# A fused attention and GEGLU block: the last accumulator of a block moved SBUF to SBUF, TensorE's lists shaped by their place in the group, dense steps shared out over a block

## The chip, the cores and the metric

One core of a Trainium2 chip runs the whole program. The metric is the device time of one execution in microseconds (us); three executions were timed, and another was profiled.

## What is computed

A transformer block on x of 2048 x 512 in float32: layer norm, attention with 32 query heads of 16 that share one key and one value head, residual; layer norm, a gated feed-forward network (F = 1792), residual.

```python
def _A_ref(x, wq, wk, wv, wo):            # attention; H = 32, Dh = 16
    q = (x @ wq).reshape(B, S, H, Dh) -> B, H, S, Dh
    k = x @ wk
    v = x @ wv
    scores = jnp.einsum("bhqd,bkd->bhqk", q, k) * (Dh ** -0.5)
    p = _softmax(scores, axis=-1)
    o = jnp.einsum("bhqk,bkd->bhqd", p, v)
    return o -> (B, S, H * Dh) @ wo
def _B_ref(x, w_gate, w_up, w_down):
    return (_gelu(x @ w_gate) * (x @ w_up)) @ w_down
h = x + _A_ref(_layernorm(x, axis=-1), A_wq, A_wk, A_wv, A_wo)
h2 = h + _B_ref(_layernorm(h, axis=-1), B_w_gate, B_w_up, B_w_down)
```

## The kernel before, and what sets its order

**Tiling.** The 2048 queries are four blocks of 512. A block has eight groups of four heads, a group has 16 chunks of 128 keys. For each chunk there are two *scores* (line 352): each is two matmuls on the two row halves of TensorE into one of two score tiles of PSUM, followed on ScalarE by one exponential of 128 x 1024 (line 356). Scores are counted here from 0 to 1023, 256 to a block. When both exponentials of a chunk are done, the chunk is *weighed* with the values (line 360): four matmuls side by side in column quarters, in float32, into the group's accumulator. The values carry a column of ones, so the accumulator holds the softmax sums too.

**Dense work.** Everything behind the attention of a block (projection pp, gate pg, up pu, down pd) is a queue of products (`queue_products`). A product is split by the two row halves of TensorE: a *step* (`step`, line 772) issues one matmul of the first half and one, six steps late (LAG), of the second half, so that the two halves work at once. Each half of a product fills one of three PSUM banks, which VectorE empties when it is complete. A queue that runs dry lets the six late second halves run alone (`catch_up`), and the next start runs six first halves alone. Block b's dense work runs beside block b + 1's attention; that of the last block follows at the end (`last_dense`). Before the last block's own products, `rest` and the projections of the first three of four column pieces stand there as filling.

**The order.** TensorE, ScalarE and GpSimd run in the order of the code, and VectorE and the SP queue too. From score 279 on the loop over CYCLES writes that order as *lists*: a list weighs 3, 3 or 2 chunks at once and then runs a string in which s is a score and d a dense step. A cycle of three lists has 8 chunks, 16 scores and 11, 11 and 14 steps. Where fewer dense steps are ready than the string has, the list is *empty*: the steps that are there are run, and then the third string of the row, which weighs one chunk (v) and takes two scores in turn. A step of a block's first products is ready when `pieces` says that its quarter of the block's output is there.

**The end of a group.** `evacuate` copies the accumulator to SBUF (oT, line 373), writes it to DRAM (acc_d, line 422) and reads it back turned (oc, line 391), both on the SP queue; only the very last accumulator goes SBUF to SBUF (line 383, SP and ScalarE's queue). At a block's last group four `piece`s follow on VectorE, one for each quarter of the queries: reciprocal, product, and a split in two float32r parts (lines 396 to 126). `outs` holds these in pairs; one pair is taken out per list.

Of the kernel before, what the change touches and what calls it, by code (L numbers as in the profile page):

```python
# [50 lines left out]
BOUND_LISTS = (3, 4)  # L51
# [6 lines left out]
def kernel(  # L58
# [12 lines left out]
    nc = tc.nc  # L71
    x = x.flatten_outer_dims()
# [7 lines left out]
    NB = S // T  # L80
# [75 lines left out]
    def run(outer, first):  # L156
# [209 lines left out]

        def take_out():
            for step in outs.pop(0):
                step()

        def evacuate(b, g, acc):
# [47 lines left out]
            if b == NB - 1 and g == NG - 1:  # L419
                move_out()  # L420
            else:
                nc.sync.dma_start(acc_d[:, g % 4, :], oT)
                if b == 0 and g < NG - 1:
                    outs.append([turn_out])
                else:
                    turn_out()
            if b == NB - 1 and g == NG - 1:
                last_out.append(piece)
            elif b > 0 and g == NG - 1:
                outs.extend([partial(piece, t), partial(piece, t + 1)] for t in (0, 2))  # L430
            elif k == 1:

                outs.extend([[] for _ in range(4 if b == 0 else 1)])
                outs.extend([partial(invert, t), partial(invert, t + 1)] for t in (0, 2))
                outs.append([divide])
            if b == 0 and g == NG - 1:
                while outs:
                    take_out()
                pieces[b] = TB
# [95 lines left out]
        clock = 0  # L535
# [27 lines left out]
        def project(b, t):  # L563
# [27 lines left out]
            return f"pp_{b}_{t}", 3 * DC, terms, done, lambda: pieces.get(b, 0) > t  # L591
# [367 lines left out]

        def finish(n):  # L960
            for _ in range(min(n, len(pend))):
                pb, pg, pkc, pp, pacc, _ = pend.pop(0)
                weigh(pacc, pp, pkc)
                if pkc == KC - 1:
                    evacuate(pb, pg, pacc)
# [35 lines left out]
        n, lead = 0, 2 * PER + 23  # L1001
        with tc.manual_schedule(engines={mybir.EngineType.SP, mybir.EngineType.DVE}):
# [25 lines left out]
            def pace():  # L1028
                nonlocal n, parts, db, tiny
# [9 lines left out]
                n += 1  # L1039
                if n % 4:  # L1040
                    return
                if outs:
# [3 lines left out]
                if n == 2 * PER + 4:  # L1046
                    prime()
# [4 lines left out]
            while n < lead:  # L1052
                pace()
                if n % 4 == 2 and len(pend) > 2 and n < lead - 1:
                    finish(1)
                elif n % 4 == 0:
                    finish(len(pend) - 2)
        assert not outs
# [8 lines left out]
        def before(idle):  # L1067
            if outs:
                take_out()
            while (b_t := divmod(sum(turned.values()), TB)) in scaled_at:  # L1070
# [19 lines left out]
        for i in range(-((lead - end) // 16)):  # L1090
            if first and i in BOUND_LISTS:
                bound_flag(BOUND_LISTS.index(i))
            for count, woven, plain in CYCLES:
                idle = available() < woven.count("d")
                if idle:
                    while available():
                        step()
                    if at == len(queue) or queue[at][0].startswith("pg"):
                        catch_up()
                bent = before(idle)  # L1100
                if not idle:
                    finish(count)
                for key in bent:
                    later.extend(gate(*key))
                for move in plain if idle else woven:
                    if move == "d":
                        step()
                    elif move == "v":
                        finish(1)
                        clock += 4  # L1110
                    elif n < end:
                        score(n)
                        n += 1
                        clock += 1
# [337 lines left out]
```

## Time and profile before

| | us |
|---|---|
| three timed executions | 1417.53, 1417.65 (median), 1420.09 |
| profiled execution, its own time | 1417.39 |
| its span, first to last instruction | 1415.2 |
| TensorE busy in the span | 1388.3 (98%) |
| ScalarE busy | 1030.1 (73%) |
| VectorE busy | 632.7 (45%) |
| first and last exponential start | 53.7 and 1263.6 |

In a row of a timeline stand start and length in us, the engine, line, operation, what it writes and reads, and how many instructions were merged; in brackets the idle time before it and what ended it. In a row of windows stand the stretch, its length, the busy time of TensorE and of its weight loads with the number of instructions (further engines where no line is picked), the granted clock, the share of the DMA engines and their GB/s. Times count from the start of the span.

### The profile page before, as it was taken

Reading aid. Unit: us, or ns where it says so; the run is one execution under the profiler, and the core shown is the slowest. Engines: PE = TensorE matmul, PEld = TensorE weight load, DVE = VectorE, ACT = ScalarE, POOL = GpSimd, SP = SyncE. Lnnn points to the kernel's source line nnn. Section 1 sums busy time; section 2 is a strip of 40 time slices with the busy share of each in tenths; the row PEclk is TensorE's granted clock in tenths of the full one; section 3 lists DMA queues with packets and bytes.
Section 4 is the critical chain, followed back from the end, with each engine's and each line's share of the span. In section 5 each row is a group of like instructions: output and inputs, shape, how many; then the busy total and the mean of one; then the engine's idle time right before and its main releaser. Section 6 shows DMA issues by size and latency. Waiting matters only on the chain.

```text
span 1415.2 us, 25089 instructions
## 1 busy us (share of the span) xinstructions
PE 1388.3 (98%) x10384; PEld 752.6 (53%) x10384; DVE 632.7 (45%) x1043; ACT 1030.1 (73%) x1147; POOL 218.3 (15%) x305
## 2 busy tenths in 40 slices
PE   6999999999999999999999999999999999999998
PEld 5533333335455555555555555545555555557886
DVE  7412221214364354454354454445264453536665
ACT  6699999997777777777777777787778777752000
POOL 5576866630000000000000000000000000001000
PEclk9999999999999999999999999999999999999999
DMA  4466766645222333311432333311333332344352
GB/s 158 135 210 204 225 211 214 213 151 199 78 85 93 116 102 117 102 65 57 153 105 87 118 116 101 102 65 36 141 101 102 117 101 102 105 141 171 131 190 77
DMA packets 66850, 180.31 MB, mean 127 GB/s; under 512 B 9484, under 2 KB 9484, under 8 KB 66696
## 3 DMA queue, kind: packets, MB, share of 16 engines
q1 hardware_dynamic: 56768, 144.40, 31.0%
q0 software_dynamic: 9760, 34.08, 7.5%
q8 instruction: 84, 1.38, 0.4%
q14 instruction: 38, 0.31, 0.1%
q10 hardware_dynamic: 200, 0.14, 0.0%
HBM read 130.87 MB, written 47.45 MB: 126 GB/s over the span
## 4 chain that ended last, share of the span: by engine, by line
PE 93%; ACT 2%; DMA 1%; DVE 1%; issue 1%; SPq 0%; DVEq 0%; ACTq 0%
PE acc L360 32%; PE s L352 20%; PE pg L772 8%; PE pu L772 8%; PE pd L772 8%; PE pq L205 4%; PE pd L802 3%; PE pp L772 2%; PE pu L802 2%; PE pg L802 2%; ACT p L356 2%; DMA w<-w_d 1%; PE pk L1240 1%; PE pd_rest L814 1%; PE pxt L598 0%
## 5 line engine op out<-in xcount | busy, mean ns | idle before, releaser
L356 ACT ACTIVATE p<-s 128x1024 f32<-128x1024 f32 x1024 | 959.3, 1040 | 231.0 <-PE s L352 230.7
L360 PE MATMUL acc<-p,v_sb 128*32 128x512 f32 x4096 | 490.0, 598 | 0.0
L352 PE MATMUL s<-qg,kaug 50*128 50x512 f32 x1984 | 386.8, 427 | 4.0 <-ACT p L356 3.6
L352 PEld LDWEIGHTS s<-qg,kaug 50*128 50x128 f32 x1984 | 170.7, 184 | 287.8 <-issue 131.3
L360 PEld LDWEIGHTS acc<-p,v_sb 128*32 128x32 f32 x4096 | 110.2, 109 | 228.9 <-issue 215.7
L772 PE MATMUL pg<-x2h,w 64*128 64x512 f32 x672 | 173.8, 392 | 0.0
L772 PE MATMUL pu<-x2h,w 64*128 64x512 f32 x672 | 172.7, 391 | 0.0
L135 POOL TENSOR_SCALAR rstd<-mv 128x1 f32<-128x1 f32 x16 | 3.5, 220 | 964.8 <-DVE mv L133 964.7
L772 PE MATMUL pd<-w,gh 64*128 64x512 f32 x624 | 123.9, 392 | 1.4 <-DVE h L702 1.4
L702 DVE TENSOR_TENSOR h<-h,pd 128x512 f32<-128x512 f32 x80 | 54.4, 686 | 148.0 <-PE pd L772 148.0
L772 PEld LDWEIGHTS pg<-x2h,w 64*128 64x128 f32 x672 | 94.3, 185 | 11.9
L772 PEld LDWEIGHTS pu<-x2h,w 64*128 64x128 f32 x672 | 94.5, 186 | 11.0
L772 PE MATMUL pg<-x2l,w 64*128 64x512 f32 x336 | 99.3, 391 | 0.0
L772 PE MATMUL pu<-x2l,w 64*128 64x512 f32 x336 | 99.1, 391 | 0.0
L772 PEld LDWEIGHTS pd<-w,gh 64*128 64x128 f32 x624 | 68.2, 185 | 13.4 <-DVE h L702 2.7
L911 ACT ACTIVATE ga<-ga 128x512 f32<-128x512 f32 x14 | 8.8, 632 | 90.4 <-DVE ga L908 90.4
L396 DVE RECIPROCAL oc<-oc 128x128 f32<-128x128 f32 x64 | 56.6, 922 | 34.5 <-DMA oc<-acc_d 27.3
L772 PE MATMUL pd<-w,gl 64*128 64x512 f32 x312 | 71.8, 391 | 0.0
L639 DVE TENSOR_TENSOR g<-g,pg 128x512 f32<-128x512 f32 x42 | 28.8, 685 | 90.5 <-PE pg L772 90.5
L635 DVE COPY g<-pg 128x512 f32<-128x512 f32 x42 | 29.0, 692 | 72.2 <-PE pg L772 72.2
L639 DVE TENSOR_TENSOR u<-u,pu 128x512 f32<-128x512 f32 x42 | 28.8, 686 | 68.3 <-PE pu L772 68.3
L373 DVE COPY oT<-acc 128x512 f32<-128x512 f32 x32 | 22.1, 691 | 72.4 <-PE acc L360 72.4
(244 smaller groups left out, 1459.2 us busy)
## 6 DMA issues: line engine op xcount, KB each, us to landing
w<-w_d SPq DMA_DIRECT2D x112, 512.0 KB
w<-w_d SPq DMA_DIRECT2D x28, 1024.0 KB
qg<-q_d SPq DMA_DIRECT2D x62, 200.0 KB
q_d<-qh SPq DMA_DIRECT2D x32, 256.0 KB
acc_d<-oT SPq DMA_DIRECT2D x31, 256.0 KB
oc<-acc_d SPq DMA_DIRECT2D x124, 64.0 KB
w_d<-w_0b POOLq DMA_DIRECT2D x14, 512.0 KB, 5.8
w_d<-w_1b POOLq DMA_DIRECT2D x14, 512.0 KB, 6.3
```

Of the source, the lines that this page charges most:

```text
L205: nc.tensor.matmul(pq, wt[:, d, c * P : (c + 1) * P], xt[:, d, :], start=(n == 0), stop=(n == 3 * DC - 1),)
L352: nc.tensor.matmul(s[:, a, :], kaug[rows, kc * P : (kc + 1) * P], qg[rows, u, :], start=True, stop=True,)
L356: nc.scalar.activation(p[:, 2 * u : 2 * u + 2, :], s, AF.Exp, scale=SCALE)
L360: nc.tensor.matmul(acc[32 * j : 32 * j + 32, :], v_sb[:, kc, :], p[:, j, :], start=(kc == 0), stop=(kc == KC - 1), skip_group_check=True,)
L373: nc.vector.tensor_copy(oT, acc)
L396: nc.vector.reciprocal(oc[:, 1, sl], oc[:, 1, sl])
L635: nc.vector.tensor_copy(half, bank)
L639: nc.vector.tensor_tensor(half, half, bank, op=ALU.add)
L702: nc.vector.tensor_tensor(hs[b, t], hs[b, t], bank, op=ALU.add)
L772: nc.tensor.matmul(bank, lhsT[r], rhs[r], start=(k == 0), stop=(k == n - 1), skip_group_check=True,)
L802: nc.tensor.matmul(bank, lhsT, rhs, start=(i == 0), stop=(i == len(ts) - 1))
L814: nc.tensor.matmul(bank, lhsT, rhs, start=(i == 0), stop=(i == len(ts) - 1))
```

## The change

1. At the last group of *every* block the accumulator goes SBUF to SBUF, by eight transfers of 16 rows on the SP and the POOL queue (the very last: SP and ScalarE's). The pieces are taken out when a count of issued work (`clock`: 1 for a step or a score, 4 for a chunk) has gone on by 30, the second pair 20 later; a quarter's projection is ready 8 and 16 counts behind that.
2. Lists are made by place in the group (`shape`): weigh runs end at chunks 3, 6 and 8 of each eight, and the string of WOVEN is picked by how many scores are then due, so there are short ones too. Where no dense steps are ready, a list weighs one chunk and takes two scores, each with up to three spare steps.
3. `spread` counts the steps left until the next block's first product and the scores left for them, and takes d out of the longest run of a string when it has more than its share. In the last block 24 steps are kept back; all that is left runs behind the last weigh run.
4. The first stage hands over at score 263 instead of 279, and the first loads of the dense work (`prime`) are issued there.

```diff
-CYCLES = (
-    (3, "ssdddddsdddsddds", "vssvssvs"),
-    (3, "ssdddddsdddsddds", "vssvssvs"),
-    (2, "ssdddddsdddsdddsddds", "ssvssvss"),
+WOVEN = (
+    "ddd", "sddd", "sdddsdd", "ssddddds", "ssdddddsddds", "ssdddddsdddsddds",
+    "ssdddddsdddsdddsddds", "ssdddddsdddsdddsdddsddds",
 )
+BOUNDARIES = ((3, 6), (6, 5), (8, 7))
+MOVE, PIECE, PAUSE = 30, 8, 20
+OPEN, KEEP = 15, 24
...
             def move_out():
+                queues = nc.sync, nc.scalar if b == NB - 1 else nc.gpsimd
                 for half in (1, 0):
                     for j in range(4):
                         r0, r1 = 64 * k + DH * j, 32 * j + DH * half
-                        (nc.sync, nc.scalar)[j % 2].dma_start(
+                        queues[j % 2].dma_start(
...
-                pieces[b] = t + 1
+                pieces[b, t] = clock + PIECE * (1 + t % 2)
...
+            if g == NG - 1:
                 move_out()
+                if b == NB - 1:
+                    last_out.append(piece)
+                else:
+                    for t in (0, 2):
+                        outs.append((clock + MOVE, [partial(piece, t), partial(piece, t + 1)]))
+                return
...
-        n, lead = 0, 2 * PER + 23
+        n, lead = 0, 2 * PER + 7
...
+        def shape():
+            m = done_chunks % 8
+            edge, extra = next(x for x in BOUNDARIES if m < x[0])
+            count = min(edge - m, len(pend))
+            aim = 2 * (done_chunks + count) + (extra if count == edge - m else n - 2 * done_chunks)
+            return count, spread(WOVEN[min(aim, end) - n])
+
+        def spread(woven):
+            todo, i = left[0], at
+            while i < len(queue) and not (todo and i in heads):
+                todo += queue[i][1]
+                i += 1
+            b = heads.index(i) if i in heads else NB - 1
+            pairs = 2 * PER * (b + 1) + OPEN - n if b < NB - 1 else end - n
+            if b == NB - 1:
+                todo -= KEEP
+            most = -(-max(todo, 0) * woven.count("s") // pairs) if pairs > 0 else len(woven)
+            while woven.count("d") > most and "ddd" in woven:
+                run = max(woven.replace("s", " ").split(), key=len)
+                woven = woven.replace(run, run[1:], 1)
+            return woven
...
+        while n < end or pend:
...
+            count, woven = shape()
+            few = available() < woven.count("d")
+            bent = before(few and not available())
+            if few:
+                count, woven = 1, None
+            finish(count)
+            clock += 4 * count
...
+            if few:
+                for _ in range(2):
+                    next_pair()
+                    spare_steps(3)
+            else:
+                for move in woven:
+                    step() if move == "d" else next_pair()
+        while available():
+            step()
```

What this does to TensorE's order is best seen in three places. First, a full list inside a block: from the second score of the list that begins with score 359 to its third (s is a score, 1 row for its two matmuls; pu_.._0 is a matmul of the first row half, for an up product, pg_.._1 one of the second half, for a gate product). Before:

```order
L352 MATMUL s_0_4379<-qg_3_3883,kaug 128x512 x2
L772 MATMUL pu_4_0_4383<-x2h_3161,w_0_4_1_4250 128x512
L772 MATMUL pg_4_1_4338<-x2h_3161,w_0_4_0_4181 128x512
L772 MATMUL pu_4_0_4383<-x2l_3162,w_0_4_1_4250 128x512
L772 MATMUL pg_4_1_4338<-x2l_3162,w_0_4_0_4181 128x512
L772 MATMUL pu_4_0_4383<-x2h_3161,w_0_4_1_4250 128x512
L772 MATMUL pg_4_1_4338<-x2h_3161,w_0_4_0_4181 128x512
L772 MATMUL pu_4_0_4383<-x2h_3161,w_0_4_1_4250 128x512
L772 MATMUL pg_4_1_4338<-x2h_3161,w_0_4_0_4181 128x512
L772 MATMUL pu_4_0_4383<-x2l_3162,w_0_4_1_4250 128x512
L772 MATMUL pg_4_1_4338<-x2l_3162,w_0_4_0_4181 128x512
L352 MATMUL s_1_4394<-qg_3_3883,kaug 128x512 x2
```

And now:

```order
L357 MATMUL s_0_4461<-qg_3_3972,kaug 128x512 x2
L777 MATMUL pu_5_0_4465<-x2h_3174,w_0_5_1_4332 128x512
L777 MATMUL pg_5_1_4420<-x2h_3174,w_0_5_0_4261 128x512
L777 MATMUL pu_5_0_4465<-x2l_3175,w_0_5_1_4332 128x512
L777 MATMUL pg_5_1_4420<-x2l_3175,w_0_5_0_4261 128x512
L777 MATMUL pu_5_0_4465<-x2h_3174,w_0_5_1_4332 128x512
L777 MATMUL pg_5_1_4420<-x2h_3174,w_0_5_0_4261 128x512
L777 MATMUL pu_5_0_4465<-x2h_3174,w_0_5_1_4332 128x512
L777 MATMUL pg_5_1_4420<-x2h_3174,w_0_5_0_4261 128x512
L357 MATMUL s_1_4474<-qg_3_3972,kaug 128x512 x2
```

Five steps have become four; the gaps behind hold three, as before. In block 1's attention from score 359 to 519 the lists are so of 10, 10 and 12 steps (in the list of 14 the gap has three). In the two later blocks, from 567 to 727 and from 844 to 1004, they are of 11, 11 and 13.

Second, TensorE at the end of block 0, around score 270. Before, lists of one weighed chunk (acc) and two scores:

```order
L360 MATMUL acc_0_3120<-p_3210,v_sb 32x512 x4
L352 MATMUL s_0_3250<-qg_0_2879,kaug 128x512 x2
L352 MATMUL s_1_3254<-qg_0_2879,kaug 128x512 x2
L360 MATMUL acc_0_3120<-p_3223,v_sb 32x512 x4
L352 MATMUL s_0_3263<-qg_0_2879,kaug 128x512 x2
L352 MATMUL s_1_3267<-qg_0_2879,kaug 128x512 x2
```

And now (the same place; pp is the first projection of block 0):

```order
L365 MATMUL acc_0_3120<-p_3222,v_sb 32x512 x4
L357 MATMUL s_1_3260<-qg_0_2879,kaug 128x512 x2
L357 MATMUL s_0_3265<-qg_0_2879,kaug 128x512 x2
L777 MATMUL pp_0_0_3269<-wo_hi,o_hi_1607 128x512
L777 MATMUL pp_0_0_3269<-wo_lo,o_hi_1607 128x512
L777 MATMUL pp_0_0_3269<-wo_hi,o_lo_1608 128x512
L777 MATMUL pp_0_0_3269<-wo_hi,o_hi_1607 128x512
L777 MATMUL pp_0_0_3269<-wo_lo,o_hi_1607 128x512
L357 MATMUL s_1_3275<-qg_0_2879,kaug 128x512 x2
```

Block 0's dense work begins at score 271 instead of 281.

Third, TensorE from the last score (s_1) on. Before, the rest of the queue stands ahead of the last weigh run, and the last block's own projection (pp) right behind it:

```order
L772 MATMUL pd_12_1_1_13188<-w_2_6_12457,gl_6_12984 128x512
L772 MATMUL pd_12_1_1_13188<-w_2_6_12457,gh_6_12983 128x512 x2
L772 MATMUL pd_12_1_1_13188<-w_2_6_12457,gl_6_12984 128x512
L360 MATMUL acc_7_12761<-p_13138,v_sb 32x512 x4
L360 MATMUL acc_7_12761<-p_13158,v_sb 32x512 x4
L857 MATMUL pp_0_13235<-wo_hi,o_hi_10935 128x512
```

And now (the first rows of 27 steps that stand between the run and pp):

```order
L357 MATMUL s_1_13137<-qg_7_12376,kaug 128x512 x2
L365 MATMUL acc_7_12739<-p_13102,v_sb 32x512 x4
L365 MATMUL acc_7_12739<-p_13125,v_sb 32x512 x4
L777 MATMUL pd_8_1_0_13160<-w_2_4_11665,gh_4_12168 128x512
L777 MATMUL pd_8_0_1_13119<-w_2_5_12514,gh_5_12730 128x512
L777 MATMUL pd_8_1_0_13160<-w_2_4_11665,gh_4_12168 128x512
L777 MATMUL pd_8_0_1_13119<-w_2_5_12514,gh_5_12730 128x512
```

The last weigh run follows its last score at once, and 27 steps have moved behind it. Counted in the whole order, the nine stretches between scores 263, 311, 359, 519, 567, 727, 791, 844, 1004 and 1024 hold 72, 105, 320, 105, 350, 132, 119, 350 and 40 steps; before, 48, 105, 360, 97, 360, 120, 119, 360 and 51. The number of matmuls is the same.

More of the change, by code (lines that the diff above doesn't have):

```diff
@@ L363, in weigh @@
                 )
+        clock = out_at = 0
         def take_out():
-            for step in outs.pop(0):
+            for step in outs.pop(0)[1]:
                 step()
@@ L534, in run @@
         tanhs, later = [], []
-        clock = 0
         def new_xT(b):
@@ L589, in done @@
                     later.append(norm)
-            return f"pp_{b}_{t}", 3 * DC, terms, done, lambda: pieces.get(b, 0) > t
+            return f"pp_{b}_{t}", 3 * DC, terms, done, lambda: (
+                (b, t) in pieces and clock >= pieces[b, t] and (b, t) in xbs
+            )
         def turn(b, t):
@@ L1053, in run @@
                 pace()
[L1054 to L1058, printed above, removed]
+            prime()
         set_banks("ps_rest")
@@ L1089, in run @@
         )
[L1090 to L1114, printed above, removed]
+        def shape():
[4 more added lines that the diff above has]
+            return count, spread(WOVEN[min(aim, end) - n])
@@ new lines, in next_pair, with spare_steps @@
+        def next_pair():
+            nonlocal n, clock
+            if n < end:
+                score(n)
+                n += 1
+                clock += 1
+        def spare_steps(k):
+            nonlocal clock
+            for _ in range(k):
+                if available():
+                    step()
+                elif ahead and (at == len(queue) or queue[at][0].startswith("pg")):
+                    step(False)
+                else:
+                    clock += 1
+                    return
@@ L1115, in run @@
+        while available():
+            step()
         fixed.close()
```

51 lines of the change are left out of this document (27 added, 24 removed).

## The prediction

> **What bounds the kernel now.** I read the page first, its busy shares and its list of waits, then the stretches of the attention phase one by one, then single lists.
>
> ```profile
> PE 1388.3 (98%) x10384; PEld 752.6 (53%) x10384; DVE 632.7 (45%) x1043; ACT 1030.1 (73%) x1147; POOL 218.3 (15%) x305
> PE s L352 <- ACT p L356: 3.6, 10, 0.6
> PE pd L772 <- DVE h L702: 1.4, 3, 0.6
> ```
>
> TensorE is busy 98% of the span. In the view of who waited for whom (us in total, times, longest), it loses 3.6 us to exponentials that are not done and 1.4 us to VectorE that has not emptied a bank. So shifting dense steps can recover some 5 us at most; it removes no matmul. The question is whether it adds waits. The next view counts the dense matmuls (L772, two to a step) in nine stretches whose ends are starts of weigh runs: those at scores 259, 311, 359, 519, 567, 727, 791, 844, 1004 and 1024.
>
> ```profile
> 304.28:364.73 60.45, 14.85 (x96) 10.26 (x96) 1.00 0.43 142
> 364.73:424.92 60.19, 30.16 (x210) 20.78 (x210) 1.00 0.25 84
> 424.92:626.25 201.33, 100.87 (x720) 69.16 (x720) 1.00 0.31 101
> 626.25:687.46 61.21, 26.96 (x194) 18.43 (x194) 1.00 0.19 57
> 687.46:888.06 200.60, 99.99 (x720) 68.50 (x720) 1.00 0.35 118
> 888.06:966.99 78.93, 34.09 (x240) 23.42 (x240) 1.00 0.22 74
> 966.99:1036.19 69.20, 33.17 (x238) 22.70 (x238) 1.00 0.33 111
> 1036.19:1236.69 200.50, 100.31 (x720) 69.02 (x720) 1.00 0.31 101
> 1236.69:1265.79 29.10, 15.09 (x102) 10.51 (x102) 1.00 0.35 116
> ```
>
> Halved, the old steps are 48, 105, 360, 97, 360, 120, 119, 360, 51: 1620. By the new order they are 72, 105, 320, 105, 350, 132, 119, 350, 40, and 27 behind the last weigh run. So 71 steps arrive (24, 8, 12 and 27) and 71 leave (40, 10, 10 and 11). What is a step worth where it arrives, and where it leaves?
>
> **A full list from the inside.** Three lists in a row on TensorE: a weigh run (acc), two scores at once, then scores with dense steps between.
>
> ```profile
> 407.51 0.73 PE L352 MATMUL s<-qg,kaug 50*128 50x512 f32 x4
> ...
> 409.24 0.42 PE L352 MATMUL s<-qg,kaug 50*128 50x512 f32 x2
> ...
> 414.18 0.73 PE L352 MATMUL s<-qg,kaug 50*128 50x512 f32 x4
> 414.75 0.40 PE L772 MATMUL pg<-x2h,w 64*128 64x512 f32 x2
> ...
> 415.90 0.46 PE L352 MATMUL s<-qg,kaug 50*128 50x512 f32 x2
> ...
> 418.18 1.92 PE L360 MATMUL acc<-p,v_sb 128*32 128x512 f32 x16
> 420.03 0.74 PE L352 MATMUL s<-qg,kaug 50*128 50x512 f32 x4
> ...
> 421.75 0.42 PE L352 MATMUL s<-qg,kaug 50*128 50x512 f32 x2
> ```
>
> Five steps fill 414.75 to 415.90: 0.23 us a step. Meanwhile ScalarE takes the exponentials, five to a row here, the five of a list:
>
> ```profile
> 408.06 4.69 ACT L356 ACTIVATE p<-s 128x1024 f32<-128x1024 f32 x5 [1.97 <-PE s L352]
> 414.78 4.69 ACT L356 ACTIVATE p<-s 128x1024 f32<-128x1024 f32 x5 [1.53 <-PE s L352]
> 420.58 4.69 ACT L356 ACTIVATE p<-s 128x1024 f32<-128x1024 f32 x5 [1.10 <-PE s L352]
> L356 ACT ACTIVATE p<-s 128x1024 f32<-128x1024 f32 x1024 | 959.3, 1040 | 231.0 <-PE s L352 230.7
> ```
>
> One takes 1.04 us, and in a row they start (4.69 - 1.04) / 4 = 0.91 us apart. There are two score tiles, so the third score of a list needs the first exponential, the fourth the second. The first ends at 408.06 + 1.04 = 409.10, and the third score starts at 409.24, 0.14 us later; in the next list 415.82 and 415.90, 0.08 later; in the third 421.62 and 421.75, 0.13 later. How close may a score follow? Here is one that TensorE had to wait for, with its exponential, the second of this row:
>
> ```profile
> 322.71 0.50 PE L352 MATMUL s<-qg,kaug 50*128 50x512 f32 x2 [0.42 <-ACT p L356]
> 320.60 2.06 ACT L356 ACTIVATE p<-s 128x1024 f32<-128x1024 f32 x2
> ```
>
> It started 0.05 us behind the exponential's end (320.60 + 2.06 = 322.66). So the five steps are no filler: they last just as long as the score must wait anyway, and with four the third score can come only 0.09, 0.03 and 0.08 us earlier. Behind it three steps and a score take 4 x 0.23 = 0.92 us, again just the 0.91 of an exponential. **A step cut from the long gap gives back some 0.07 us, not 0.23; the rest becomes a wait.** The second step cut from the same gap gives nothing.
>
> **The change part by part.**
> - *Steps that leave full lists.* Scores 359 to 519: ten cycles with 10, 10 and 12 steps for 11, 11 and 14, each 0.09 + 0.03 + 0.08 = 0.2 us shorter: -2.0. In the two stretches of -10 only the list of 14 loses one: ten times 0.08, -0.8 each. Scores 311 to 359: three such, -0.2. Bounds for these 63 cuts: nothing given back (0) and all of it (63 x 0.23 = -14.5); I take the 3.8 that the three lists show.
> - *Steps that arrive.* At the first block end 24 x 0.23 = 5.5; there the lists of one weigh chunk and two scores, with no dense steps, become fewer. At the second 8 x 0.23 = 1.8. At the third 12 x 0.23 = 2.8, and eight more that were cut in that stretch's full lists and sit in its formerly empty ones, 8 x 0.16 = 1.3. Lists at the first and second end that are cut too: +0.9 of waits. Bounds: none of it hidden (as here), or half of it where a score waited.
> - *Waits that go.* What TensorE lost around the first end (305 to 372), the second (618 to 640; two rows) and the third (936 to 960; two rows):
>
> ```profile
> PE s L352 <- ACT p L356: 2.1, 5, 0.6
> PE s L352 <- ACT p L356: 0.4, 1, 0.4
> PE pd L772 <- DVE h L702: 0.3, 1, 0.3
> PE s L352 <- ACT p L356: 0.9, 3, 0.5
> PE pd L772 <- DVE h L702: 0.5, 1, 0.5
> ```
>
>   Half of the first stays, since six of twelve lists without dense steps stay: -1.0; at the second -0.7, at the third -1.4, together -3.1. Starts of weigh runs cancel: 157 lists before, 157 after.
> - *The end.* Rows of TensorE around the last weigh run, and the last place where it waits for VectorE's quarters:
>
> ```profile
> 1262.61 0.72 PE L772 MATMUL pd<-w,gh 64*128 64x512 f32 x3 [0.55 <-DVE h L702]
> ...
> 1265.79 1.92 PE L360 MATMUL acc<-p,v_sb 128*32 128x512 f32 x16
> 1267.65 0.50 PE L857 MATMUL pp<-wo_hi,o_hi 128*128 128x512 f32 x1
> ...
> 1281.92 0.50 PE L857 MATMUL pp<-wo_hi,o_hi 128*128 128x512 f32 x1 [0.29 <-DVE o_hi L125]
> ```
>
>   The last list loses seven steps, six unpaired half steps (three slots) and a wait: 10 x 0.23 + 0.55 = -2.9; the three lists before it -0.2. Behind the run stand 27 steps and the three slots: 30 x 0.23 = +6.9. The weigh run then waits for its last exponential, +0.5 (a score and its exponential less one chunk of 0.9). Six-step products side by side empty banks fast, and the last FFN chunk is projected only just ahead: +1.0, from 0 to 3. What they cover is little: TensorE works without a gap from 1267.65, and the quarters cost it 0.3 to 0.6: -0.5.
> - *SBUF to SBUF.* What the two routes take from the copy of the accumulator to the first reciprocal:
>
> ```profile
> 620.72 0.69 DVE L373 COPY oT<-acc 128x512 f32<-128x512 f32 x1 [1.28 <-PE acc L360]
> 627.38 0.95 DVE L396 RECIPROCAL oc<-oc 128x128 f32<-128x128 f32 x1 [0.20 <-issue]
> 1267.79 0.69 DVE L373 COPY oT<-acc 128x512 f32<-128x512 f32 x1 [1.20 <-PE acc L360]
> 1273.97 0.95 DVE L396 RECIPROCAL oc<-oc 128x128 f32<-128x128 f32 x1 [5.50 <-DMA oc<-oT]
> ```
>
>   5.97 us through DRAM, 5.49 directly. In the new order the quarters stand on VectorE where a count is reached, later than that at the second and third end (two lists, some 13 us); at the first they stand about where the data lands. I take 0; bounds -0.5 and, if the POOL queue is slow, +3 once. The Trainium skill, "DMA: Bandwidth & Descriptors", section "Anatomy of one DMA — SWDGE (gpsimd) path", gives each DMA a fixed cost of about 2.0 us; by it one leg less would be worth 2.0 at each of three ends, and the sum below would be an estimated 6 lower; the trace shows 0.5 between the routes.
> - *Two quarters at once between bank evictions.* The third quarter's reciprocal begins 3.57 us behind the first's:
>
> ```profile
> 630.95 0.94 DVE L396 RECIPROCAL oc<-oc 128x128 f32<-128x128 f32 x1
> ```
>
>   So a pair holds VectorE 3.6 us beside products that need banks; before, empty lists lay there. Bounds 0 and 2.5 at each of two ends; I take 0, since the products' steps are spaced by scores.
>
> **The sum:** leaving -2.0 - 0.8 - 0.8 - 0.2 = -3.8; arriving 5.5 + 1.8 + 2.8 + 1.3 + 0.9 = +12.3; waits -3.1; end -3.1 + 6.9 + 0.5 + 1.0 - 0.5 = +4.8. Together +10.2, less about 1 for the three or four arriving steps that fall into a score's wait (0.4 and 0.6 us in the rows above): **+9**. The profiled execution took 1417.39 us, so 1426.4; the median of the runs is 0.26 above it: **1426.6 us**, 0.6% slower.
>
> **The rivals.**
> 1. *The score could start earlier* (faster). If the third score followed its exponential by less than the 0.05 us seen, or exponentials ran faster with less beside them, a cut step would give back all of 0.23. It decides from a margin of 0.23 behind the exponential; the lists show 0.14, 0.08 and 0.13. Then leaving is -14.5, the waits that I put at 0.9 and 1.3 go, and the sum is -14.5 + 10.1 - 3.1 + 4.8 - 1 = -3.7: 1414.0. Against it: every one of the three lists. Chance 0.08.
> 2. *Half of that*: cut steps give back half, 1420 or so. Chance 0.09.
> 3. *New waits at the block ends*: quarters before evictions, a late POOL transfer or the last FFN chunk stall TensorE by 2.5 + 2.5 + 3 more: 1431 to 1435. For it: VectorE's 3.6 us; against it: 1.4 us of bank waits in the whole span. Chance 0.13.
> 4. *The clock falls.* The new waits come in nearly every list. In the first stretch TensorE waited most and its granted clock stood at 1.00, as in the others. The Trainium skill, "TensorE: Matmul & The Clock Gate", section "A second HAM failure mode: psum-queue depth-cycling", tells of frequent short idle times between groups that threw the clock between half and full; the trace does not agree, waits of up to 0.6 us left it at 1.00. Half a clock in the third stretch alone would add its 201 us. Chance under 0.01.
>
> **How the numbers follow.** The forecast, 1421 to 1431, has 0.69. The range reaches down to the half case and up into the third rival: 1418 to 1433, with about 0.83 inside. A measurement of this kernel tells 0.2% (2.8 us) from no change, so faster is below 1414.8 and slower above 1420.5. Faster: three quarters of the first rival, 0.06. Within: the rest of it and most of the second, 0.10. Slower: the forecast, the third and fourth and what is left of the second, 0.84.
>
> **What would show it.** In the new profile the scores' wait for exponentials should grow from 3.6 us to some 10, in many pieces of 0.1 to 0.2 between scores 359 and 519; a cycle there should last 19.8 to 19.9 us with four steps fewer, against 20.05 (200.50 us for ten in the stretch from 1036.19); the last weigh run should start some 4 us later, and the work behind it 5 to 7 us later still. If a cycle lasts 19.1, the first rival is right; if waits for VectorE grow by several us, the third.

## The result

The changed kernel takes 1435.49 us (median of 4 runs, 1433.06 to 1438.52) for 1417.7 us before: ratio 1.0123, 95% interval 1.0100 to 1.0145. It is 1.2% slower. The forecast was 1426.6 us with a range up to 1433, so the direction was right and the size was half of what came. The profiled execution took 1436.32 us (span 1434.5, granted clock 0.997).

### The profile after

The page's busy line, and then, from the view of who waited for whom (us in total, times, longest), the lines that answer to those of before:

```profile
PE 1405.6 (98%) x10384; PEld 753.1 (53%) x10384; DVE 639.3 (45%) x1052; ACT 1030.8 (72%) x1147; POOL 224.3 (16%) x317
```

```profile
PE s L357 <- ACT p L361: 4.6, 20, 0.6
PE pd L777 <- DVE gh L674: 1.0, 1, 1.0
PE pd L777 <- DVE h L707: 0.5, 1, 0.5
```

TensorE runs the same 10384 matmuls and is busy 17.3 us longer; its waits as this view counts them hardly grew. So the loss isn't where that view looks. It is found by stretches: the dense matmuls (L777) between the starts of the same weigh runs as before (scores 259, 311, 359, 519, 567, 727, 791, 844, 1004, 1024), with the length of each stretch in the second column and the granted clock in the third from the right:

```profile
303.56:369.83 66.27, 23.27 (x144) 15.64 (x144) 1.00 0.40 133
369.83:430.02 60.19, 29.48 (x210) 20.18 (x210) 1.00 0.29 93
430.02:630.19 200.17, 90.88 (x640) 60.54 (x640) 1.00 0.29 95
630.19:694.09 63.90, 29.64 (x210) 20.44 (x210) 1.00 0.17 50
694.09:894.83 200.74, 98.07 (x700) 67.25 (x700) 1.00 0.34 115
894.83:975.40 80.57, 37.36 (x264) 25.23 (x264) 1.00 0.25 80
975.40:1045.66 70.26, 33.66 (x238) 22.95 (x238) 1.00 0.32 105
1045.66:1246.19 200.53, 98.17 (x700) 67.06 (x700) 1.00 0.30 99
1246.19:1271.95 25.76, 11.27 (x80) 7.58 (x80) 1.00 0.21 69
```

Set against the nine stretches of before:

| stretch (scores) | steps | change, us |
|---|---|---|
| up to 259 | none | -0.72 |
| 259 to 311 | 48 to 72 | +5.82 |
| 311 to 359 | 105, 3 lists cut | 0.00 |
| 359 to 519 | 360 to 320 | -1.16 |
| 519 to 567 | 97 to 105 | +2.69 |
| 567 to 727 | 360 to 350 | +0.14 |
| 727 to 844 | 239 to 251 | +2.70 |
| 844 to 1004 | 360 to 350 | +0.03 |
| 1004 to 1024 | 51 to 40 | -3.34 |
| last weigh run to the end | 0 to 27 | +13.14 (149.41 to 162.55) |

Together +19.3, the difference of the two spans. Two things stand out: 60 steps left three stretches that got 0.99 us shorter between them, and the end, with 6.2 us of steps in it (27 x 0.23), got 13 longer.

### What a cut list looks like

The stretch that lost 40 steps, one list of 10 (four steps, three, three) on TensorE, and the exponentials beside it (rows left out are marked ...):

```profile
430.02 2.78 PE L365 MATMUL acc<-p,v_sb 128*32 128x512 f32 x24
432.73 0.73 PE L357 MATMUL s<-qg,kaug 50*128 50x512 f32 x4
...
434.35 0.49 PE L357 MATMUL s<-qg,kaug 50*128 50x512 f32 x2
...
435.38 0.40 PE L357 MATMUL s<-qg,kaug 50*128 50x512 f32 x2
...
436.30 0.40 PE L357 MATMUL s<-qg,kaug 50*128 50x512 f32 x2
```

```profile
433.27 4.69 ACT L361 ACTIVATE p<-s 128x1024 f32<-128x1024 f32 x5 [1.47 <-PE s L357]
```

The first exponential ends at 433.27 + 1.04 = 434.31 and the third score starts 0.04 behind it: it waits now, as forecast. It comes 1.62 us after the list's first score; in the list of 11 at 407.51 it was 1.73. That is 0.11 won. But the next gap, three steps and a score as ever, is 435.38 - 434.35 = 1.03 us long. Before, it was 0.92, from the third score at 409.24 to the fourth:

```profile
410.16 0.45 PE L352 MATMUL s<-qg,kaug 50*128 50x512 f32 x2
```

Look at the rows' own lengths: the score that waited takes 0.49 us where its neighbours take 0.40. It takes 0.1 us longer, and everything behind it comes 0.1 us later; that is called a restart here. **What the cut gives, the restart takes.** No bracket stands at 434.35: a wait of this size shows as a longer row and a longer gap, not as idle time.

### The end

TensorE from the last weigh run to the block's own projection (pp):

```profile
1271.95 2.43 PE L365 MATMUL acc<-p,v_sb 128*32 128x512 f32 x16
1274.31 0.76 PE L777 MATMUL pd<-w,gh 64*128 64x512 f32 x4
...
1277.62 0.45 PE L777 MATMUL pd<-w,gl 64*128 64x512 f32 x2
1279.04 0.73 PE L777 MATMUL pd<-w,gh 64*128 64x512 f32 x4 [0.98 <-DVE gh L674]
...
1280.11 0.39 PE L777 MATMUL pd<-w,gh 64*128 64x512 f32 x1
1281.05 0.73 PE L777 MATMUL pd<-w,gh 64*128 64x512 f32 x3 [0.55 <-DVE h L707]
...
1285.94 0.79 PE L862 MATMUL pp<-wo_hi,o_hi 128*128 128x512 f32 x1
```

The first fifteen steps take 0.23 us each. Then TensorE waits for the last FFN chunk (gh). VectorE at that time:

```profile
1274.43 0.69 DVE L380 COPY oT<-acc 128x512 f32<-128x512 f32 x1 [1.93 <-PE acc L365]
1276.04 0.69 DVE L707 TENSOR_TENSOR h<-h,pd 128x512 f32<-128x512 f32 x1 [0.92 <-PE pd L777]
1276.64 0.68 DVE L662 SCALAR_TENSOR_TENSOR ga<-ga,g 128x512 f32<-128x512 f32 x1
...
1278.57 0.42 DVE L674 CAST gh<-ga 128x512 fp32r<-128x512 f32 x1
```

The chunk stands behind the copy of the last accumulator, which itself waits 1.93 us, and behind two additions (the second, at 1277.97, is left out above). And then, in windows of two microseconds (columns: PE, PEld, DVE, ACT, POOL busy, granted clock, DMA share, GB/s), the clock falls:

```profile
1278.00:1280.00 2.00, 1.02 (x8) 0.53 (x7) 1.68 (x4) 0.00 (x0) 0.00 (x0) 1.00 0.88 259
1280.00:1282.00 2.00, 1.45 (x11) 0.84 (x11) 1.28 (x2) 0.00 (x0) 0.00 (x0) 0.92 0.11 24
1282.00:1284.00 2.00, 2.00 (x9) 1.61 (x6) 0.93 (x2) 0.00 (x0) 0.00 (x0) 0.50 0.64 129
...
1288.00:1290.00 2.00, 2.00 (x10) 1.62 (x9) 1.86 (x6) 0.00 (x0) 0.00 (x0) 0.87 0.16 58
```

From about 1281.7 to 1288.5 it stands at half, some 6.8 us, of which half is lost.

### The profile page after: what moved, and what is told of

Same layout as the page of the kernel before. It is cut to its first block, busy times and chain, and to the rows that moved or that the text cites. A ratio compares the mean times of both kernels' runs of the same rounds, so it can differ in the third digit from the quotient of the medians.

```text
span 1434.5 us, 25146 instructions
## 1 busy us (share of the span) xinstructions
PE 1405.6 (98%) x10384; PEld 753.1 (53%) x10384; DVE 639.3 (45%) x1052; ACT 1030.8 (72%) x1147; POOL 224.3 (16%) x317
## 4 chain that ended last, share of the span: by engine, by line
PE 92%; ACT 2%; DVE 2%; DMA 1%; issue 1%; POOL 0%; DVEq 0%; ACTq 0%; POOLq 0%
PE acc L365 32%; PE s L357 21%; PE pu L777 8%; PE pg L777 8%; PE pd L777 7%; PE pq L210 3%; PE pd L807 3%; ACT p L361 2%; PE pu L807 2%; PE pg L807 2%; PE pp L777 2%; PE pp L862 1%; DMA w<-w_d 1%; PE pd_rest L819 1%; PE pxt L603 1%
## 5 line engine op out<-in xcount | busy, mean ns | idle before, releaser
L357 PE MATMUL s<-qg,kaug 50*128 50x512 f32 x1984 | 392.3, 432 | 5.2 <-ACT p L361 4.6
L777 PE MATMUL pg<-x2h,w 64*128 64x512 f32 x672 | 175.6, 392 | 0.0
L777 PE MATMUL pu<-x2h,w 64*128 64x512 f32 x672 | 175.5, 392 | 0.0
L777 PE MATMUL pd<-w,gh 64*128 64x512 f32 x624 | 121.2, 396 | 1.7 <-DVE gh L674 1.0
L707 DVE TENSOR_TENSOR h<-h,pd 128x512 f32<-128x512 f32 x80 | 54.4, 687 | 149.4 <-PE pd L777 149.3
L777 PEld LDWEIGHTS pu<-x2h,w 64*128 64x128 f32 x672 | 94.5, 186 | 11.8
L777 PEld LDWEIGHTS pg<-x2h,w 64*128 64x128 f32 x672 | 94.5, 186 | 10.9
L777 PE MATMUL pg<-x2l,w 64*128 64x512 f32 x336 | 99.4, 392 | 0.0
L777 PE MATMUL pu<-x2l,w 64*128 64x512 f32 x336 | 99.2, 392 | 0.0
L391 POOL DMA_DIRECT2D oc<-oT x12 | 6.0, 503 | 546.4 <-DVE oT L380 546.4
L777 PEld LDWEIGHTS pd<-w,gh 64*128 64x128 f32 x624 | 68.7, 187 | 15.0 <-DVE gh L674 1.4
L777 PE MATMUL pd<-w,gl 64*128 64x512 f32 x312 | 72.3, 396 | 0.0
L130 DVE CAST qh<-pq 128x512 fp32r<-128x512 f32 x11 | 7.6, 690 | 110.6 <-PE pq L210 110.6
```

The costliest lines, as they stand in the source:

```text
L357: nc.tensor.matmul(s[:, a, :], kaug[rows, kc * P : (kc + 1) * P], qg[rows, u, :], start=True, stop=True,)
L707: nc.vector.tensor_tensor(hs[b, t], hs[b, t], bank, op=ALU.add)
L777: nc.tensor.matmul(bank, lhsT[r], rhs[r], start=(k == 0), stop=(k == n - 1), skip_group_check=True,)
```

## The experiments

My theory (A): a step cut from a full list gives nothing back, a step costs 0.23 us where it arrives, and the end pays for two waits and a fallen clock behind them. The rival (B): a step is worth 0.23 us wherever it stands, so the cuts do give back, and the loss comes from the clock or from new waits at the block ends. The kernel before took 1418.16 us (9 runs) beside e1 to e4, 1417.08 (7 runs) beside e5 to e8 and 1420.22 (one run) beside e9 to e12.

### e1: one step moved within each list of the kernel before

```
-    (3, "ssdddddsdddsddds", "vssvssvs"),
+    (3, "ssddddsddddsddds", "vssvssvs"),
```

(and the same in the other two lists)

> The kernel before, with one dense step of every full list moved from the gap of five (between the second and the third score) to the gap of three behind it, so that lists read 4, 4, 3 for 5, 3, 3 and 4, 4, 3, 3 for 5, 3, 3, 3. The number of steps, weigh runs and scores stays. Theory A, from the two traces (a gap of five is just the wait of the third score, a step cut from it gives back 0.10 us, and the score that then waits makes the next gap 0.10 us longer): the step costs nothing where it was and 0.13 to 0.23 us where it goes, so some 140 lists add 18 to 32 us: 1436 to 1450, and a cycle lasts 20.45 to 20.75 us for 20.05. Theory B (a step is worth 0.23 us wherever it stands): no change, 1417 to 1419, cycle 20.05.

Measured: 1448.9 us, ratio 1.0221 (1.0205 to 1.0236), +30.7. Nine cycles from score 359 on, before and with the step moved:

```profile
424.92:605.41 180.49, 90.31 (x648) 62.08 (x648) 1.00 0.32 105
```

```profile
428.38:614.88 186.50, 90.14 (x648) 61.52 (x648) 1.00 0.31 102
```

The same 324 steps take 6.01 us more in 27 lists, 0.22 each. One such list:

```profile
431.10 0.73 PE L352 MATMUL s<-qg,kaug 50*128 50x512 f32 x4
...
432.72 0.49 PE L352 MATMUL s<-qg,kaug 50*128 50x512 f32 x2
...
433.96 0.40 PE L352 MATMUL s<-qg,kaug 50*128 50x512 f32 x2
```

The gap of four is 1.62 us long, as in the changed kernel, and the score behind it takes 0.49; the gap that got a fourth step is 1.24 instead of 0.92. The step costs nothing where it was and its full length where it went, restart included. B falls.

### e2: the changed kernel without cuts

```
-            return count, spread(WOVEN[min(aim, end) - n])
+            return count, WOVEN[min(aim, end) - n]
```

> The changed kernel without the cutting of full lists: every list keeps 11 or 14 steps, so the steps of the first block run out before the second end (7 lists without steps come before it, 4 behind it, 4 at the third), and 10 steps for 27 stand behind the last weigh run. Theory A (cut steps give nothing back): the full cycles last as long as with cuts, 20.05 us, and the places where the cut steps stood become shorter: stretch 359 to 519 about -5 us, second and third end -3, behind the last weigh run -17 x 0.23 = -3.9, and the two waits there (1.5) and the half clock (3.3) go: about 1420, from 1417 to 1424. Theory B (a cut step gives back 0.23): the steps are only moved, so about -2 to -5 for what goes behind the last weigh run: 1431 to 1434.

Measured: 1425.04 us (1424.92 to 1427.4), ratio 1.0054 (1.0041 to 1.0068). That is 10.5 below the changed kernel, far from B, and about 1 above A's range (1417 to 1424). The uncut lists of the next block cost nothing: the stretch from 567 to 727 takes 200.81 us with 360 steps, for 200.74 with 350:

```profile
691.52:892.33 200.81, 100.18 (x720) 68.31 (x720) 1.00 0.36 117
```

From 359 to 567 it is 4.8 us shorter (259.30 for 264.07), and from the last weigh run to the end 153.3 for 162.6. What A had missed is the third end, where TensorE now waits 2.8 us for VectorE:

```profile
PE pd L777 <- DVE gh L674: 1.6, 1, 1.6
PE pp L777 <- DVE x2l L609: 0.6, 1, 0.6
PE pd L777 <- DVE h L707: 0.6, 1, 0.6
```

There the third rival of the prediction happens, in a kernel that runs out of steps earlier.

### e3: 14 of the 27 last steps back into full lists

```
-OPEN, KEEP = 15, 24
+OPEN, KEEP = 15, 0
```

> The changed kernel with 13 steps behind the last weigh run instead of 27; 14 cut steps go back into full lists behind score 844. Theory A: the 14 cost nothing there and 3.2 us less at the end; the two waits for VectorE at the end (0.98 and 0.55 us) and the half clock behind them (some 3.3 us in the profiled execution) go: -6 to -8, 1427 to 1430. Theory B (cut steps gave back 0.23 each): only the waits and the clock: -3 to -5, 1430 to 1433. If the half clock stays, both are 3 higher.

Measured: 1429.97 us (1429.27 to 1430.27), ratio 1.0084 (1.0070 to 1.0098). The stretch from 844 to 1004:

```profile
1047.15:1247.64 200.49, 100.07 (x720) 68.34 (x720) 1.00 0.31 102
```

360 steps in 200.49 us, where the changed kernel takes 200.53 for 350: ten steps for nothing. The end takes 154.6 us for 162.6, with one wait (0.55, h) and the clock at 1.00. The total stands at the edge between the two ranges (1427 to 1430 and 1430 to 1433); it is the stretch that decides for theory A.

### e4: the last FFN chunk ahead of the last accumulator

```
+            if n >= end:
+                for key in bent:
+                    later.extend(gate(*key))
+                bent = ()
+                side(100)
             finish(count)
```

> The changed kernel with one thing in another order: in the last pass VectorE makes gh and gl of the last FFN chunk (four instructions) before it copies the last accumulator, not behind it and two additions. All 27 steps stay. Theory A (the clock falls because TensorE waited twice within 3 us, 0.98 and 0.55 us): both waits go or shrink to under 0.3, the granted clock stays at 1.00, -3.5 to -5: 1430 to 1432. Theory B (the clock falls for another reason, the dense steps of six-term products side by side): only the waits go, -1 to -1.5, and the clock still reads 0.50 for some us: 1434 to 1435.

Measured: 1433.44 us (1432.89 to 1433.99), ratio 1.0110 (1.0094 to 1.0125). The wait for gh is gone, but the additions stand later, so that TensorE waits 0.33 and 0.55 us for h. The time lies in neither range (A 1430 to 1432, B 1434 to 1435): the clock is as A has it, the gain is not. The clock stays up:

```profile
1280.00:1282.00 2.00, 1.45 (x13) 0.86 (x11) 1.28 (x2) 0.00 (x0) 0.00 (x0) 1.00 1.02 410
1282.00:1284.00 2.00, 2.00 (x13) 1.47 (x9) 1.29 (x2) 0.00 (x0) 0.00 (x0) 1.00 0.82 255
```

### e5: the changed kernel again

No edit.

> The changed kernel once more, as the base of the three others and to see whether the half clock at the end comes again. Theory A (it follows from the two waits of 0.98 and 0.55 us, which are in the order of the instructions): the waits come again, and the clock reads 0.50 for several us behind them; 1433 to 1438. Theory B (chance of the one execution): the waits come again and the clock stays at 1.00: the profiled execution takes about 1433.

Measured: 1435.92 us (1434.58 to 1437.62). The two waits and the half clock come again, this time for some 10.2 us; the end takes 163.8 us.

### e6: the last accumulators through DRAM again

```
-                move_out()
                 if b == NB - 1:
+                    move_out()
                     last_out.append(piece)
                 else:
+                    nc.sync.dma_start(acc_d[:, g % 4, :], oT)
+                    turn_out()
```

> The changed kernel with its first part undone: the last accumulators of the first three blocks go through DRAM again, on SyncE's queue; the order of TensorE's instructions stays. Theory A (the transfer is off the path, since the quarters wait for a count anyway): no change against the changed kernel on the same chip, within 1 us. Theory B (the direct transfer saved a fixed cost at each of three ends): +1.5 to +6 us.

Measured: 1436.86 us (1434.78 to 1438.19) beside 1435.92 for e5: no difference that these runs can tell. Scores 256 to 1023 take 10.0 us more than before, 9.5 in e5; most of the difference is one step at score 619, between block ends. At the three ends themselves the two agree within 0.1 us (259 to 311 +5.75 and +5.77, 519 to 567 +2.66 in both, 727 to 791 +1.64 in both). The transfer is off the path. What this run shows besides: the same two waits of 0.98 and 0.54 us at the end, and no fall of the clock behind them.

```profile
1280.00:1282.00 2.00, 1.02 (x8) 0.52 (x7) 1.69 (x4) 0.00 (x0) 0.00 (x0) 1.00 0.95 280
1282.00:1284.00 2.00, 1.46 (x11) 0.89 (x11) 1.28 (x2) 0.00 (x0) 0.00 (x0) 1.00 0.13 26
1284.00:1286.00 2.00, 2.00 (x13) 1.34 (x9) 1.28 (x2) 0.00 (x0) 0.00 (x0) 1.00 0.87 229
```

### e7: dense work from score 279, as before

```
-        n, lead = 0, 2 * PER + 7
+        n, lead = 0, 2 * PER + 23
...
+                if n > 2 * PER + 7:
+                    finish(len(pend) - 2)
+                if n == 2 * PER + 4:
+                    prime()
```

> The changed kernel with the dense steps of the first block starting at score 279 as in the kernel before, not at 263; scores 264 to 279 stand behind two weigh chunks each. 158 steps for 177 stand between scores 259 and 359, and the 19 others go back into full lists between 359 and 519. Theory A (a step costs 0.23 us where it arrives and nothing in a full list): -3.5 to -4.4 against the changed kernel, all of it before score 359: 1431 or so. Theory B (0.23 us wherever it stands): within 1 us of the changed kernel.

Measured: 1432.08 us (1431.71 to 1432.19), ratio 1.0107 (1.0090 to 1.0124). From score 259 to 359, the changed kernel first and then e7:

```profile
303.56:430.02 126.46, 52.75 (x354) 35.82 (x354) 1.00 0.35 114
```

```profile
303.71:428.73 125.02, 47.27 (x316) 31.50 (x316) 0.99 0.34 108
```

19 steps fewer save 1.4 us here, not the 3.5 to 4.4 of A. Two things lie between. The clock falls here, after two waits for exponentials:

```profile
307.18 0.50 PE L357 MATMUL s<-qg,kaug 50*128 50x512 f32 x2 [0.66 <-ACT p L361]
308.10 0.50 PE L357 MATMUL s<-qg,kaug 50*128 50x512 f32 x2 [0.41 <-ACT p L361]
308.53 3.30 PE L365 MATMUL acc<-p,v_sb 128*32 128x512 f32 x16
```

```profile
307.00:309.00 2.00, 1.41 (x8) 0.53 (x12) 0.00 (x0) 2.00 (x4) 1.72 (x4) 0.98 0.29 63
309.00:311.00 2.00, 2.00 (x16) 0.43 (x8) 0.17 (x1) 1.79 (x2) 0.32 (x1) 0.50 0.61 103
```

which costs 1.6 us: the weigh run of four chunks takes 3.30 us where the next one of four takes 1.92, and the three scores behind it 1.22 for 0.97. And from 303 to 374 us TensorE waits 3.6 us for exponentials where it waited 2.0. Without the fall the 19 steps are worth 3.1 us, 0.16 each: where lists hold no steps, a part of what a step costs is a wait that it fills. In full lists the 19 steps are free again: scores 359 to 519 take 200.36 us with 339 steps, for 200.17 with 320.

```profile
428.73:629.09 200.36, 95.40 (x678) 64.64 (x678) 1.00 0.32 100
```

That the whole time is 3.8 below e5, as A asked, is in part luck: the end of the profiled e7 takes 159.0 us without a fall of the clock there, that of e5 163.8 with one.

### e8: whole lists at the block ends

```
-            few = available() < woven.count("d")
+            few = available() < min(6, woven.count("d"))
...
-                    step() if move == "d" else next_pair()
+                    if move == "s":
+                        next_pair()
+                    elif available():
+                        step()
```

> The changed kernel with whole lists at the block ends: a list is short only where fewer than 6 steps are there, else it keeps its shape and leaves out the steps that are not there. 6 weigh runs fewer (15 for 17 at the first end, 10 for 12 at the second, 12 for 13 and 10 for 11 at the third and behind it), the steps stand within 4 of where they stood. Theory A (the stretch behind score 791 got 1.06 us longer with the same 119 steps because one list was split in two): 0.5 to 1.0 us for each split, -3 to -6. Theory B (only the steps count): within 1 us.

Measured: 1435.95 us (1433.86 to 1437.67), the same as e5. The third end and the stretch behind it, 727 to 844, get 0.35 shorter (150.48 for 150.83), the second 1.2 longer (65.07 for 63.90). The theory of the split list falls here: that a list is short costs nothing that these runs can tell. The half clock comes again at the end (163.3 us).

### e9 to e12: the changed kernel and e4, twice more each

No edit in e9 and e10; e11 and e12 are e4 again.

> One more look at the changed kernel (no edit), for the clock at its end. So far the half clock stood there in three of five executions of kernels that have both waits (0.98 and 0.55 us), and in none of five without the longer one. Theory A (the two waits bring it on, not each time): it reads 0.50 again, with a chance of some 0.6. Theory B (it has to do with something else that comes and goes): it comes as often in the other order of VectorE's instructions.

> As the look before it: the changed kernel, no edit. Theory A: the half clock with a chance of some 0.6, and then the work from the last weigh run to the end takes 162 to 164 us, else 159.

> One more look at the kernel that makes gh and gl of the last FFN chunk before it copies the last accumulator. Theory A: waits of 0.3 and 0.55 us, the clock at 1.00, and 158 us from the last weigh run to the end. Theory B: the half clock here too, with a chance of some 0.6.

> As the look before it, the same kernel. Theory A: the clock at 1.00. Theory B: the half clock with a chance of some 0.6; if it comes in neither look, theory B is left with a chance of 0.4 x 0.4 x 0.4 for three executions without it.

Measured: 1434.83, 1432.52, 1434.96 and 1434.65 us. None shows the half clock at the end, though e9 and e10 have the two waits. All executions together, from the start of the last weigh run to the end of the span:

| kernel | waits at the end, us | clock there | last weigh run to end, us |
|---|---|---|---|
| before, e1 | 0.3 | 1.00 | 149.4, 150.4 |
| after, e5, e8 | 0.98 and 0.55 | falls to 0.50 | 162.6, 163.8, 163.3 |
| e6, e7, e9, e10 | 0.98 and 0.55 | 1.00 | 158.7, 159.0, 159.2, 159.1 |
| e4, e11, e12 | 0.33 and 0.55 | 1.00 | 158.2, 159.1, 159.5 |
| e3 | 0.55 | 1.00 | 154.6 |
| e2 | 0.73 | 1.00 | 153.3 |

The fall costs 3.6 to 4.8 us against the mean of 159.0 and comes in three of seven executions with both waits, in none of seven with less. The waits without the fall are not what costs: e4's order takes as long as the other. The spread of the changed kernel's times goes with the clock too: its three timed executions took 1433.06, 1434.66 and 1438.52 us at mean granted clocks of 0.999, 0.998 and 0.994.

Why three of seven? The moments at which the granted clock changes, in us of each trace:

| execution | clock rises first | falls | rises again | falls once TensorE has ended |
|---|---|---|---|---|
| after | 22.16 | 1281.68 | 1288.51 | 1431.87 |
| e5 | 21.99 | 1281.51 | 1291.75 | 1431.69 |
| e8 | 21.98 | 1281.50 | 1291.74 | 1431.69 |
| e7 | 22.21 | 308.93 | 312.34 | 1428.50 |
| e6 | 22.71 | 60.26 | 63.67 | 1429.00 |

All differences within a row, and in the other traces, are whole multiples of 3.413 us: in the first, 1259.52 is 369 of them, 6.83 is 2 and 143.36 is 42. So the clock is set once in a window of that length, and where the windows lie differs from one execution to the next. The Trainium skill, "TensorE: Matmul & The Clock Gate", section "What's actually happening", gives a free-running window of 3413 ns; the trace agrees. Now add up, per window, the time by which matmuls at the end start later than 0.23 us behind the one before. In the window that ends with the fall that is 1.95 us (after), 2.15 (e5) and 2.00 (e8): both stops lie in it. In e6, e7, e9 and e10 the fullest window holds 1.50, 1.18, 1.18 and 1.73, since a boundary runs through the pair. In e4's order it is 1.28, 1.16 and 0.99, and its two stops with what goes with them make some 1.4 us, less than 1.73 wherever the windows lie. The limit is between 1.73 and 1.95 of 3.41 us by this count. The two stops with what goes with them make some 2.2 us in the changed kernel, so its clock falls or not by where the windows lie. At the first end the same count fails (2.01 us in a window of the changed kernel that kept 1.00, 2.00 in the one of e7 that didn't), because a weighed chunk takes 0.41 us until the next start, not 0.23. With 0.41 behind a chunk the count can be made over all 14 traces, from the clock's first rise to the last matmul: 5730 whole windows at full clock, and eleven falls, one in e7, three at the end and seven early in a trace (six at about 60 us, one in e12 at 14.5). The eleven windows lost 1.87 to 2.24 us; of all others two lost more than 1.87 (1.99 and 1.95, both kept 1.00), the rest 1.84 or less. The first end of the changed kernel comes to 1.71, that of e7 to 1.87. So it is one limit everywhere in these traces, near 1.9 of 3.41 us, known to some 0.1. No run was made to set it.

## Why the prediction was wrong

The direction, the steps of each stretch and the mechanism of the third score were right. The size failed: the sum was +9.2, the spans differ by 19.3. Two steps of the prediction make most of that: what a step cut from a full list gives back (3.6 us), and the end behind the last weigh run (5.2 us, most of it a fall of the clock that had a chance of under 0.01).

- **Steps that leave full lists: -3.8 forecast, -0.2 measured** (0.00, -0.36 for nine of the ten cycles, +0.14, +0.03). This is the first step that failed: "A step cut from the long gap gives back some 0.07 us, not 0.23". The score that was made to wait was timed rightly; I didn't follow the list on to the next score, which comes 0.10 us later because the score that waited takes 0.10 us longer. The row for it stood in the prediction: the score at 322.71, which waited, takes 0.50 us, those at 409.24 and 415.90, which did not, 0.42 and 0.46 (two matmuls that start a little apart, each of 0.40 at 409.24). I read its start and not its length. e1 and e3 show the same from both sides.
- **Steps that arrive, waits that go and what falls into waits: 12.3 - 3.1 - 1 = +8.2 forecast, +10.4 measured.** The third end came out as forecast, +2.7, in part by luck, since its waits shrank from 1.4 to 0.8 us and not to nothing. The second is +1.9 (its tenth cycle's wait gone, -0.8, counted in) against some +1.5. The first is +5.8 against some +4: the waits there shrank only from 2.3 to 2.0 us, not by half. At the three ends together the waits that the view shows went from 4.4 to 3.2, -1.2 for the -3.1 of the sum: that is most of this miss.
- **The end up to the last weigh run: -3.1 forecast, -3.34 measured.**
- **Behind it: +7.9 forecast, +13.1 measured.** This is the second step that failed, "+1.0, from 0 to 3" for the last FFN chunk and nothing for the clock. Without the fall of the clock it is +9.6 (159.0 - 149.4). The two stops, where I put 1.0 within 0 to 3, make some 0.9 of that excess of 1.7: counted from the starts of the rows and a step's 0.23 us they last 1279.04 - 1277.85 = 1.2 and 1281.05 - 1280.34 = 0.7 us, more than the idle time shown, since a row's modelled length runs past its 0.23. Nearly all of the other 0.8 is restarts, which the sum has at nothing: in e9, whose clock stays up, seven starts from the weigh run to the second of the projection come 0.09 to 0.16 us later than a step's 0.23, some 0.8 us together; before, one does. The fall makes 3.6. The fourth rival had it under 0.01 and looked for it in the lists with many small waits; it came at the end, after two longer ones close together. The Trainium skill, "TensorE: Matmul & The Clock Gate", section "A second HAM failure mode: psum-queue depth-cycling", tells of a kernel in which frequent short idle times between groups make the clock swing between half and full. The prediction found the trace of before against it; here the clock does fall, once, to 0.50 for 6.8 us, where 1.95 us of one window of 3.413 were lost.
- **Before score 259: -0.7**, the same within 0.1 in e5, while e1 to e4 and e6 are 0.7 to 0.9 us over before at this place: a difference between executions: their clock falls for one window at about 60 us.

These misses come to 3.6 + 2.2 + 5.2 - 0.2 - 0.7 = 10.1.

**SBUF to SBUF at 0 was right** (e6): its block ends agree with those of e5 within 0.1 us, where e6's theory B had +1.5 to +6 in all. The 5.97 us through DRAM in the prediction is an upper bound, since the reciprocal at 627.38 waited for no transfer ([0.20 <-issue]). The sign of the whole was right too: a slower kernel, since no step was removed and the cut ones came from places where they were free. Of the third rival's waits, that for the last FFN chunk came in the changed kernel (0.98 us at its end); those at the block ends came only in e2.

The signs that the prediction asked for failed in part: it asked for 10 us of scores' waits in the view of waits, and the view shows 4.6. Waits of 0.1 us are longer rows there (mean 432 ns for 427), not idle time. The last weigh run was to start some 4 us later and the work behind it 5 to 7 later still, where the prediction's own sum gives 1.3 and 7.9; 6.2 and 13.1 came. The cycle, "19.8 to 19.9 us", is 180.13 / 9 = 20.01:

```profile
430.02:610.15 180.13, 81.78 (x576) 54.49 (x576) 1.00 0.29 96
```

No version here beats the kernel before. Without cuts (e2) it still takes 7 us more: it loses 6.4 us between scores 259 and 359, where the first block's work starts earlier, 3.1 between 727 and 844, where it waits for VectorE, and 3.9 behind the last weigh run, and wins some of it back between.

## What to carry over

Work that fills a wait exactly is free, and it stops being free in any other place; before you even out a resource over a phase, ask of each place that gives whether it gets shorter, and follow the chain past the next dependent instruction, since a wait costs its own length and a restart. Read that restart from the length of a row that waited beside one that did not. At the end of a kernel, look at what stands ahead of the last producer on its engine, and look at the granted clock behind waits that come close together.

## What was not expected of the hardware

A matmul of 512 columns that had to wait takes 0.49 to 0.50 us where one in a stream takes 0.39 to 0.40, and the stream behind it is 0.10 us later (e1, the cut lists). The granted clock falls to 0.50 without any long idle time: at the end no single stop was longer than 1.2 us, but 1.95 to 2.15 us were lost in one window of 3.413 us. Over all 14 traces the windows that ended in a fall lost 1.87 to 2.24 us, and only two others lost more than 1.87. The clock then stays down for one, two or three whole windows (3.41, 6.83 and 10.24 us).
